# Cosine of h in the first feed-forward: one shifted sine in place of a half-angle sine and its square

## The chip, the cores and the metric

The kernel runs on one core of one Trainium2 chip, in one launch. The metric is device time in microseconds (us), lower is better. The engines are TensorE (PE in the profile, with its weight loads shown apart as PEld), VectorE (DVE), ScalarE (ACT), GpSimd (POOL) and SyncE (SP, which issues most of the DMAs). The kernel before takes 839.35 us, the median of 3 runs (838.67 to 839.87).

## The reference, cut to what matters

The input goes through attention (pooled and local, added up), then two feed-forward blocks. What the change touches is the middle of the first one:

```python
def _moe_ref(x, w_in, w_out):          # x: 2304 x 512, w_in: 512 x 2048, w_out: 2048 x 512
    h = x @ w_in
    g = h * np.cos(h)
    return (g @ w_out).astype(np.float32)
```

The second block computes `(x @ w1) * (x @ w2) @ w3 @ w_out`. All of it is float32.

## The kernel before, in words

**The order of the work is made by a planner, not by hand.** The body of the kernel is written as jobs (Python generators); each step of a job asks for an engine, and `run` (L294) plays a clock of its own: it keeps for each engine the planned end of its last operation, and whenever an engine is free it issues the most urgent step whose inputs are, by the plan, visible. What an operation costs is a formula in `cost` (L104), what it takes until its output can be read is the table `LATENCY`. For ScalarE the formula is (L113 to L115):

```python
load = 1290 if func in (AF.Exp, AF.Sin) and func != table[0] else 0
table[0] = func if load else table[0]
return (45 if not on_chip(ins[0]) else 128 if func == AF.Prelu else 90) + n / 1.2 + load
```

so a 384-column operation costs 365 (in ns) from a PSUM bank and 410 from SBUF, whatever the function, scale and bias. The program that results has one fixed order on every engine; on the chip each engine takes its instructions in that order, and waits where an input is not there yet. A changed cost or a step less can therefore change the order of everything that is issued after it, on all engines.

**The first feed-forward.** 2304 tokens are 6 chunks of 384 columns (N1), the hidden 2048 are 16 blocks of 128 (F1): 96 steps. Every float32 matrix product is made of three passes in the float32r format (a high and a low part of each operand, `mm3`). A step is 12 matmuls for h (`h_job`, L856) into one PSUM bank, then the chain that makes g of it (`chain_job`, L836), then 12 matmuls for y (`y_job`, L883), which add into four banks over the 16 blocks. `LAG = 3` (L56, used in L865) lets h run three steps ahead of y. With the last block of a chunk `y_out_job` (L907) writes y out through ScalarE with `scale=-1.0`, because the chain leaves minus g. There are 32 such copies, as the first two chunks are made in two parts.

**The chain of a step** before the change:

1. ACT: `turns` = h / 2pi as an int32 (rounded)
2. DVE: `c` = h - 2pi * turns
3. ACT: `c` = sin(c / 2)
4. ACT: `c` = (sqrt(2) * c) squared, which is 1 - cos h
5. DVE: `c` = (c - 1) * h, which is -h cos h; the PSUM bank of h is free after it
6. ACT: the high part of g, a copy of `c` as float32r
7. POOL: the low part of g, `c` minus the high part

**Around it.** The start loads and converts the weights (ACT and DVE), does the attention of the first batch and multiplies w3 by w4 of the second block (`ps_w`). From 82 us on the steps of the first feed-forward run, with the attention of the later chunks strewn between them on PE (tiles `ps_s`, `ps_t`, `ps_p`, `ps_sb`, `ps_tb`, `ps_av`). At 557 us the second feed-forward begins (`ps_ab`, `ps_o`); it has no chain. Dummy matmuls that keep PE going (`warm_up`) stop at the first step of h. The first instructions of POOL are memsets of constants (in the block that begins at L1087, the last of them at L1125, `ge.memset(ident, 0.0)`); the four DMAs of the band masks and the two of the identity are issued from ACT's queue.

Of the kernel before, what the change touches and what calls it, by code (L numbers as in the profile page):

```python
# [10 lines left out]
F32 = mybir.dt.float32  # L11
# [4 lines left out]
AF = mybir.ActivationFunctionType  # L16
ALU = mybir.AluOpType
# [5 lines left out]
P = 128  # L23
# [31 lines left out]
TWO_PI = 2.0 * math.pi  # L55
# [24 lines left out]
def fused_kernel(ctx: ExitStack, tc: tile.TileContext, qk_block, v_block, qk_pool, v_pool,  # L80
# [84 lines left out]
    ve, se, pe, ge, sy = (Engine(*e) for e in (("ve", nc.vector), ("se", nc.scalar), ("pe", nc.tensor), ("ge", nc.gpsimd), ("sy", nc.sync)))  # L165
# [8 lines left out]
    const = ctx.enter_context(tc.tile_pool(name="const", bufs=1))  # L174
# [8 lines left out]
    ident = const.tile([P, P], F32, name="ident")  # L183
    ident_r = const.tile([P, P], F32R, name="ident_r")
    bands = const.tile([P, 3, 2 * KS], F32R, name="bands")


    slots = {"t": (tp, 2048, 6), "st": (tp, 4096, 1), "g": (gp, 8 * N1, 3), "c": (gp, 4 * N1, 2), "turns": (gp, 4 * N1, 1),
# [8 lines left out]
    def buf(slot, name, shape, dtype=F32):  # L197

        pool, size, _ = slots[slot[0]]
        item = 8 if dtype == I64 else 4  # L200
        t = pool.tile([P, size // item], dtype, name=name, tag=f"{slot[0]}{slot[1]}", bufs=1)
        t = t[:, :math.prod(shape)]
        if len(shape) == 1:
            return t
        names = "abcd"[:len(shape)]
        return t.rearrange(f"p ({' '.join(names)}) -> p {' '.join(names)}", **dict(zip(names, shape)))
# [6 lines left out]
    def bank(n, name):  # L213

        return psum.tile([P, 512], F32, name=name, tag=f"bank{n}", bufs=1)
# [18 lines left out]
    def on(name, fn, *aps, when=lambda: True):  # L234
        yield name, fn, aps, when
# [5 lines left out]
    def at_hand(name):  # L241
        return sorted(x for x in free[name] if x[0] <= now[0])

    def take(name, n=1, spare=lambda: 0):

        yield from until(lambda: len(at_hand(name)) >= n + spare())
        got = at_hand(name)[:n]
        for x in got:
            free[name].remove(x)
        return got[0][1] if n == 1 else [x[1] for x in got]  # L250
# [15 lines left out]
    def give(name, slot, engine):  # L266
        free[name].append((ends[engine] + LATENCY[engine], slot))

    def give_stored(name, slot, to):

        free[name].append((visible(to), slot))

    def count(key, n=1):
        done[key] = done.get(key, 0) + n

    def reached(key, n):
        return lambda: done.get(key, 0) >= n
# [558 lines left out]
    def chain_job(n, ps, at):  # L836

        turns_slot = yield from take("turns")
        turns = buf(turns_slot, "turns", [N1], I32)
        yield from on("se", lambda: se.activation(out=turns, in_=ps, func=AF.Identity, scale=1.0 / TWO_PI), ps)  # L840
        c_slot = yield from take("c")
        c = buf(c_slot, "c", [N1])
        yield from on("ve", lambda: ve.scalar_tensor_tensor(out=c, in0=turns, scalar=-TWO_PI, in1=ps, op0=ALU.mult, op1=ALU.add), turns)
        give("turns", turns_slot, "ve")
        yield from on("se", lambda: se.activation(out=c, in_=c, func=AF.Sin, scale=0.5), c)
        yield from on("se", lambda: se.activation(out=c, in_=c, func=AF.Square, scale=math.sqrt(2.0)), c)
        yield from on("ve", lambda: ve.scalar_tensor_tensor(out=c, in0=c, scalar=1.0, in1=ps, op0=ALU.subtract, op1=ALU.mult), c)
        give("bank", at, "ve")
        g_slot = yield from take("g")
        g = buf(g_slot, "g", [2, N1], F32R)  # L850
        yield from on("se", lambda: se.copy(g[:, 0, :], c), c)
        yield from on("ge", lambda: ge.tensor_tensor(out=g[:, 1, :], in0=c, in1=g[:, 0, :].bitcast(F32), op=ALU.subtract), g)
        give("c", c_slot, "ge")
        gs[n] = g, g_slot
# [52 lines left out]
    def y_out_job(i, f, e, ps):  # L907
        slot = yield from take("t")
        yt = buf(slot, "yt", [N1])
        yield from on("se", lambda: se.activation(out=yt, in_=ps, func=AF.Copy, scale=-1.0), ps)  # L910
        give(f"bank{4 + e}", 0, "se")
        to = (y_sc if f == F1 - 1 else part_sc)[:, e, i * N1:(i + 1) * N1]
        yield from on("se", lambda: se.dma_start(out=to, in_=yt), yt)
        give_stored("t", slot, to)
        count("stored")
# [171 lines left out]
    with tc.manual_schedule():  # L1087
        z = buf(("turns", 0), "zeros", [WARM])
        ge.memset(z, 0.0)
        zr = z.bitcast(F32R)  # L1090
        warmed = [(bank(7, "ps_z"), True)]

        def warm_up():

            if warmed[0] is None:
                if done.get("w5", 0) < F2 or not at_hand("bank7"):
                    return False
                ps, alone = bank(7, "ps_z"), True
            else:
                ps, alone = warmed[0]  # L1100
            pe.matmul(ps[:, :WARM], lhsT=zr[:, :P], rhs=zr, start=alone, stop=alone)
            ends["pe"] += REST if now[0] > RISEN else 0
            return True

        idle.append(warm_up)

        W5 = 2 * F2
        first, seen = {}, []
        first.update({i: HALF if i == 1 else F1 * i for i in range(NC1)})
        first.update({("f", f): f if f < HALF else f + HALF for f in range(F1)})  # L1110

        def attention(i, at):

            for b in sorted({(UPC * i + m) // UPB for m in range(UPC)} - set(seen)):
                seen.append(b)
                if b < EARLY:
                    for m in range(UPB):
                        Job(at + U_QK + 0.5 * m, unit_qk_job(UPB * b + m))
                for p in range(KC):
                    Job(at + U_PAIR + SLOPE * p, pair_job(b, p))  # L1120
                    Job(at + U_POOL + SLOPE * p, pool_v_job(b, p))
            for m in range(UPC):
                Job(at + U_UNIT + PER_UNIT * m, unit_job(UPC * i + m))

        ge.memset(ident, 0.0)  # L1125
        raw = buf(("st", 0), "bands_raw", [3, 2, KS])
        for half in (slice(0, KS), slice(KS, P)):
            for w in range(2):
                se.dma_start(out=raw[half, :, w], in_=bands_in[w * (QB - KS):, :, w * (KB - KS):][:KS, :, :KS])
        se.dma_start(out=ident[:QB, :QB], in_=ident_in)  # L1130
        se.dma_start(out=ident[QB:, QB:], in_=ident_in[:P - QB, :P - QB])

        se.activation(out=ident_r[:, :1], in_=z[:, :1], func=AF.Exp)
        Job(-50, consts_job(raw))
        ends["sy"] = FIRST
        attention(0, A0)
        for j in range(F2):
            at = j - 1 if j >= 2 else -5.75 + 0.02 * j
            Job(at, w_job(("w4", j), w4[j]))
            Job(at + (0.5 if j >= 2 else 0.01), w_job(("w3", 0, j), w3t[0, j]))  # L1140
        for j in range(F2):
            Job(F2 + j + U_W3, w_job(("w3", 1, j), w3t[1, j]))
        Job(900, w5_job())
        for f in range(F1):
            Job(W5 + first["f", f] + U_WI, w_job(("wi", f), w_in[f]))
            Job(W5 + first["f", f] + U_WO, w_job(("wo", f), w_out[f]))
        Job(899, h_job(W5))
        Job(W5 + 1000.5, y_job())
        attention(1, W5 + first[1] - A1)
        for i in range(2, NC1):  # L1150
            run(reached("h", first[i - 1] + 1 - AHEAD if i > 2 else first[0] + HALF + 1))
            attention(i, W5 + first[i])
            if i == 2:
                for f in range(F2):
                    Job(W5 + first[2] + 4 * f, w12_job(f))
        run(lambda: done.get("h", 0) > first[NC1 - 1] and done.get("w12 begun", 0) == F2)
        at_stack.close()
        p2 = ctx.enter_context(tc.tile_pool(name="p2", bufs=1))
        slots.update({"x2": (p2, 4 * KC * N1, 6), "v": (p2, 4 * NH, 2)})
        free["x"] += [(0.0, ("x2", n)) for n in range(6)]  # L1160
        free["v"] = [(0.0, ("v", n)) for n in range(2)]
        base = W5 + NSTEPS
        for n in range(F2 * NQ // 2):
            Job(base + 2 * n / NQ - 8, back_job(n))
        for n in range(len(steps2)):
            Job(base + n - 6, w5_back_job(n))
        Job(base - 8, y_in_job(0))
        Job(base + 1000, ab_job(base))
        Job(base + 1000.5, o_job(base))
        run(reached("out", NT // P))  # L1170
# [53 lines left out]
```

## Time and profile before

| | |
|---|---|
| median of 3 runs | 839.35 us (838.67 to 839.87) |
| the profiled execution | 842.03 us, of which the span of its records is 840.2 us |
| PE busy, PEld busy | 825.3 us (98%), 750.2 us (89%) |
| DVE, ACT, POOL busy | 512.4 us (61%), 464.2 us (55%), 325.6 us (39%) |
| first h, last y of the first feed-forward | 82 us, 557 us |

How to read it: "busy" is the time in which an instruction of an engine runs. Matmuls overlap, and their ends are modelled, so PE's busy time says that it had something, not how fast it went; the steady pace of its groups says that. Idle time "<-X" in front of an instruction is what it waited for. Almost every instruction has the line L161, that of the planner's helper, so groups are told apart by the names of the tiles. In every stretch the granted TensorE clock is 1.00 of full speed.

### The profile page before, as it was taken

What the parts mean: (1) busy time and instruction counts of PE and PEld (TensorE: products, weight loads), DVE (VectorE), ACT (ScalarE), POOL (GpSimd) and SP (SyncE); (2) the same over time, 40 slices, a digit from 0 to 9 for tenths busy, and PEclk for the clock granted to TensorE, in tenths of its full rate; (3) what the DMA queues carried; (4) which work ended last, traced back from release to release, by engine and by line L of the source; (5) the groups of instructions that cost most, each with busy time, mean ns of one, the idle gap of its engine ahead of it and who ended that gap; (6) DMA issues with size and microseconds to landing.
All of it is one profiled execution on the core that took longest, in us unless ns stands there. A gap on an engine that the chain in (4) does not pass through costs nothing.

```text
span 840.2 us, 15590 instructions
## 1 busy us (share of the span) xinstructions
PE 825.3 (98%) x5972; PEld 750.2 (89%) x5972; DVE 512.4 (61%) x935; ACT 464.2 (55%) x930; POOL 325.6 (39%) x298
## 2 busy tenths in 40 slices
PE   7999999999999999999999999999999999999997
PEld 6545669999899999999999999999999999999996
DVE  4988989997775989467453436424336544463342
ACT  3788988876886787767666566631114311331112
POOL 0103214334362654534543324425336633363332
PEclk9999999999999999999999999999999999999999
DMA  9999896144445653353232258870000510120102
GB/s 286 298 304 299 306 329 214 44 138 132 167 132 171 201 175 107 128 191 126 85 136 89 94 191 347 283 255 14 26 26 14 175 26 26 26 95 20 26 25 76
DMA packets 48923, 121.88 MB, mean 145 GB/s; under 512 B 6480, under 2 KB 10832, under 8 KB 48848
## 3 DMA queue, kind: packets, MB, share of 16 engines
q1 hardware_dynamic: 41952, 112.12, 40.7%
q10 hardware_dynamic: 6896, 8.76, 2.9%
q8 instruction: 47, 0.77, 0.4%
q14 instruction: 28, 0.23, 0.1%
HBM read 93.07 MB, written 27.79 MB: 144 GB/s over the span
## 4 chain that ended last, share of the span: by engine, by line
PE 81%; DVE 8%; DMA 4%; ACT 3%; issue 2%; POOL 0%; ACTq 0%; SPq 0%; DVEq 0%; POOLq 0%
PE ps_ab L161 21%; PE ps_y L161 20%; PE ps_h L161 20%; PE ps_o L161 12%; PE ps_w L161 2%; DVE t L161 2%; DMA raw<-w3t 2%; PE ps_av L161 1%; DVE c L161 1%; PE ps_t L161 1%; PE ps_tb L161 1%; PE ps_sb L161 1%; PE ps_s L161 1%; DMA vr<-v_pool 1%; DVE sc L161 1%
## 5 line engine op out<-in xcount | busy, mean ns | idle before, releaser
L161 PE MATMUL ps_y<-g,wo 128*128 128x384 f32 x1152 | 221.9, 337 | 0.0
L161 PE MATMUL ps_h<-xs,wi 128*128 128x384 f32 x1152 | 221.5, 337 | 0.0
L161 PEld LDWEIGHTS ps_h<-xs,wi 128*128 128x128 f32 x1152 | 200.4, 188 | 3.8 <-issue 3.2
L161 PEld LDWEIGHTS ps_y<-g,wo 128*128 128x128 f32 x1152 | 199.8, 188 | 3.0 <-issue 2.1
L161 PE MATMUL ps_ab<-y,w 128*128 128x384 f32 x1008 | 189.0, 337 | 0.4 <-ACT v L161 0.3
L161 POOL TENSOR_TENSOR g<-c,g 128x384 fp32r<-128x384 f32 x96 | 106.7, 1112 | 206.5 <-ACT g L161 192.1
L161 PEld LDWEIGHTS ps_ab<-y,w 128*128 128x128 f32 x1008 | 177.5, 188 | 8.5 <-POOL v L161 0.9
L161 DVE TENSOR_TENSOR v<-v,ps_ab 128x384 f32<-128x384 f32 x168 | 90.8, 552 | 141.8 <-PE ps_ab L161 74.0
L161 ACT ACTIVATE c<-c 128x384 f32<-128x384 f32 x192 | 100.4, 523 | 42.9 <-DVE c L161 39.0
L161 ACT CAST m<-v 128x384 fp32r<-128x384 f32 x48 | 24.6, 513 | 176.8 <-POOL v L161 176.8
L161 PE MATMUL ps_o<-w,m 128*128 128x512 f32 x432 | 110.9, 393 | 0.0
L161 POOL TENSOR_TENSOR v<-v 128x384 f32<-128x384 f32 x48 | 50.5, 1054 | 126.8 <-DVE v L161 126.8
L161 DVE SCALAR_TENSOR_TENSOR c<-turns,ps_h 128x384 f32<-128x384 int32 x96 | 52.7, 549 | 66.3 <-ACT turns L161 59.3
L161 PEld LDWEIGHTS ps_o<-w,m 128*128 128x128 f32 x432 | 80.1, 188 | 12.5
L161 DVE SCALAR_TENSOR_TENSOR c<-c,ps_h 128x384 f32<-128x384 f32 x96 | 52.7, 549 | 54.6 <-ACT c L161 54.3
L161 ACT CAST g<-c 128x384 fp32r<-128x384 f32 x96 | 49.0, 511 | 38.9 <-DVE c L161 34.4
L161 PE MATMUL ps_w<-w,w 128*128 128x512 f32 x128 | 61.0, 607 | 1.7 <-DVE w L161 1.6
L161 ACT ACTIVATE turns<-ps_h 128x384 int32<-128x384 f32 x96 | 46.7, 486 | 27.3 <-PE ps_h L161 27.1
L161 POOL TENSOR_TENSOR m<-v,m 128x384 fp32r<-128x384 f32 x48 | 49.1, 1025 | 23.7 <-ACT m L161 23.7
L161 POOL TENSOR_TENSOR sc<-sc,bmax 128x1024 f32<-128x1024 f32 x12 | 23.6, 1966 | 68.9 <-DVE bmax L161 52.6
L161 PEld LDWEIGHTS ps_w<-w,w 128*128 128x128 f32 x128 | 22.4, 189 | 23.5 <-issue 19.9
L161 DVE SCALAR_TENSOR_TENSOR t<-raw,t 128x512 int32<-128x512 int32 x48 | 42.8, 902 | 0.2
(90 smaller groups left out, 861.9 us busy)
## 6 DMA issues: line engine op xcount, KB each, us to landing
w_sc<-w SPq DMA_DIRECT2D x56, 256.0 KB, 2.3
w<-w_sc SPq DMA_DIRECT2D x28, 512.0 KB, 6.9
raw<-w SPq DMA_DIRECT2D x24, 512.0 KB, 11.9
qk<-qk_block SPq DMA_DIRECT2D x24, 396.0 KB, 8.5
raw<-w3t SPq DMA_DIRECT2D x16, 512.0 KB, 13.5
raw<-w_in SPq DMA_DIRECT2D x16, 512.0 KB, 7.5
raw<-w_out SPq DMA_DIRECT2D x16, 512.0 KB, 8.5
qkr<-qk_pool SPq DMA_DIRECT2D x12, 576.0 KB
```

The source lines that it names most:

```text
L161: return call(*args, **kw)
```

## The change

The argument of the sine is no longer halved. The turns are counted from a quarter turn on (a bias of 0.25 ahead of the rounding), so the rest lies between -3/4 and 1/4 of a turn; with a bias of a quarter turn in the sine it lies between -1/2 and 1/2, and sin(rest + pi/2) is cos h. The square goes away, the second DVE operation becomes a plain product of two tensors, and y is written with the sign as it is. The two biases are columns of a new tile `quarters`, filled by two memsets at the start of POOL's program.

```diff
+    quarters = const.tile([P, 2], F32, name="quarters")
...
     turns = buf(turns_slot, "turns", [N1], I32)
-    yield from on("se", lambda: se.activation(out=turns, in_=ps, func=AF.Identity, scale=1.0 / TWO_PI), ps)
+    yield from on("se", lambda: se.activation(out=turns, in_=ps, func=AF.Identity, scale=1.0 / TWO_PI, bias=quarters[:, 1:]), ps)
...
     give("turns", turns_slot, "ve")
-    yield from on("se", lambda: se.activation(out=c, in_=c, func=AF.Sin, scale=0.5), c)
-    yield from on("se", lambda: se.activation(out=c, in_=c, func=AF.Square, scale=math.sqrt(2.0)), c)
-    yield from on("ve", lambda: ve.scalar_tensor_tensor(out=c, in0=c, scalar=1.0, in1=ps, op0=ALU.subtract, op1=ALU.mult), c)
+    yield from on("se", lambda: se.activation(out=c, in_=c, func=AF.Sin, bias=quarters[:, :1]), c)
+    yield from on("ve", lambda: ve.tensor_tensor(out=c, in0=c, in1=ps, op=ALU.mult), c)
...
-    yield from on("se", lambda: se.activation(out=yt, in_=ps, func=AF.Copy, scale=-1.0), ps)
+    yield from on("se", lambda: se.activation(out=yt, in_=ps, func=AF.Copy, scale=1.0), ps)
...
+    ge.memset(quarters[:, :1], TWO_PI / 4)
+    ge.memset(quarters[:, 1:], 0.25)
     ge.memset(ident, 0.0)
```

## Rows read from the trace of the kernel before

**Rows 1.** Stretches of the span: length, busy time (instructions) of each engine, clock, DMA

```profile
0.00:82.00 82.00, 74.58 (x715) 46.20 (x716) 61.64 (x126) 58.06 (x138) 13.44 (x13) 1.00 0.97 296
82.00:123.00 41.00, 39.28 (x249) 26.92 (x247) 36.80 (x76) 37.38 (x80) 8.51 (x6) 1.00 0.85 311
123.00:190.00 67.00, 66.33 (x560) 64.88 (x557) 65.60 (x111) 54.91 (x108) 23.91 (x18) 1.00 0.43 144
190.00:345.00 155.00, 154.57 (x1498) 144.87 (x1497) 118.73 (x232) 118.53 (x226) 76.31 (x67) 1.00 0.49 156
345.00:557.00 212.00, 212.00 (x1516) 209.91 (x1515) 104.53 (x177) 130.56 (x261) 87.59 (x83) 1.00 0.50 172
557.00:840.00 283.00, 278.53 (x1446) 257.46 (x1444) 125.14 (x219) 64.75 (x121) 115.81 (x112) 1.00 0.16 51
```

**Rows 2.** Waits of PE from 82 to 345 us, and from 557 us on (last row)

```profile
PE ps_p L161 <- DVE vd L161: 1.7, 1, 1.7
PE ps_tb L161 <- POOL sc L161: 0.7, 1, 0.7
PE ps_t L161 <- DVE sc L161: 0.2, 1, 0.2
...
PE ps_ab L161 <- ACT v L161: 0.3, 2, 0.2
```

**Rows 3.** Chain that ended last, two groups of PE and the end of the last steps

```profile
441.41 2.08 PE ps_y L161 x12
443.49 2.08 PE ps_h L161 x12
...
549.57 8.32 PE ps_y L161 x48
```

**Rows 4.** Groups of instructions by form: ACT and DVE (count, busy us, mean ns)

```profile
L161 ACT ACTIVATE c<-c 128x384 f32<-128x384 f32 x192 | 100.4, 523 | 42.9 <-DVE c L161 39.0 <-DVE t L161 1.5
L161 ACT ACTIVATE turns<-ps_h 128x384 int32<-128x384 f32 x96 | 46.7, 486 | 27.3 <-PE ps_h L161 27.1
L161 ACT ACTIVATE yt<-ps_y 128x384 f32<-128x384 f32 x32 | 14.8, 489 | 9.1 <-ACT yt L161 4.4 <-PE ps_y L161 3.3 <-PE ps_ab L161 0.8
L161 ACT ACTIVATE sd<-ps_s,nm 72x144 f32<-72x144 f32 x32 | 11.6, 370 | 1.1 <-DVE nm L161 1.1
L161 ACT ACTIVATE up<-ps_t 128x144 f32<-128x144 f32 x12 | 3.5, 294 | 0.0
L161 DVE SCALAR_TENSOR_TENSOR c<-c,ps_h 128x384 f32<-128x384 f32 x96 | 52.7, 549 | 54.6 <-ACT c L161 54.3
L161 DVE TENSOR_TENSOR v<-v,ps_ab 128x384 f32<-128x384 f32 x168 | 90.8, 552 | 141.8 <-PE ps_ab L161 74.0 <-ACT w L161 66.0 <-POOL y L161 0.9
```

**Rows 5.** Sines and squares from 82 to 190 us (ACT, groups by form)

```profile
L161 ACT ACTIVATE c<-c 128x384 f32<-128x384 f32 x38 | 19.9, 523 | 3.6 <-DVE c L161 1.5 <-DVE t L161 1.5
```

**Rows 6.** Timeline of the last chain, with PE's last y of the stage (start us, us)

```profile
549.41 8.48 PE L161 MATMUL ps_y<-g,wo 128*128 128x384 f32 x48
...
550.35 0.48 ACT L161 ACTIVATE turns<-ps_h 128x384 int32<-128x384 f32 x1
551.52 1.08 ACT L161 ACTIVATE c<-c 128x384 f32<-128x384 f32 x2 [0.69 <-DVE c L161]
553.94 1.01 POOL L161 TENSOR_TENSOR g<-c,g 128x384 fp32r<-128x384 f32 x1 [1.42 <-ACT g L161]
```

**Rows 7.** Timeline of the start: POOL's memsets, ACT's queue

```profile
0.34 0.10 POOL L1217 MEMSET const-uint8-127<- 128x1 uint8 x1
0.98 0.20 POOL L161 MEMSET ident<- 128x128 f32 x1
3.40 1.44 ACTq L147 DMA_DIRECT2D ident<-ident_in  x2
```

**Rows 8.** Timeline of the two longest waits of PE after 82 us

```profile
120.88 0.69 DVE L161 TENSOR_TENSOR vr<-vr 72x512 f32<-72x512 f32 x1 [2.78 <-DMA vr<-v_pool]
122.51 0.71 PE L161 MATMUL ps_p<-ptp,vd 72*64 72x144 f32 x8 [1.72 <-DVE vd L161]
...
183.83 0.52 ACT L161 CAST g<-c 128x384 fp32r<-128x384 f32 x1 [1.14 <-DVE c L161]
184.48 1.02 POOL L161 TENSOR_TENSOR g<-c,g 128x384 fp32r<-128x384 f32 x1 [6.02 <-ACT g L161]
185.45 2.14 POOL L161 TENSOR_TENSOR sc<-sc,bmax 128x1024 f32<-128x1024 f32 x1
187.65 1.09 PE L161 MATMUL ps_tb<-ident,sc 128*128 128x128 f32 x8 [0.67 <-POOL sc L161]
```

## The prediction

> **What bounds the kernel now.** I read the stretches first, then the waits of PE, then the chain that ended last. Up to 82 us the transfers are the limit: the DMA engines are busy 0.97 of the time [rows 1], and no step of h has begun, so no chain runs there. From 82 us on it is PE. Its idle time, length less busy time, is 1.72 us from 82 to 123, 0.67 from 123 to 190, 0.43 from 190 to 345 and nothing at all from 345 to 557 [rows 1]. Busy time of PE is modelled, so I check the pace too: in the steady part the chain that ended last is twelve matmuls of y, twelve of h, and so on, 2.08 us each and back to back [rows 3]; nothing but PE stands on it. What PE waits for behind 82 us adds up to 1.7 + 0.7 + 0.2 + 0.3 = 2.9 us [rows 2]. That is the whole sum that relief on ACT, or anything else beside PE, can win there unless PE's own work falls, and the change leaves every matmul as it is.
>
> **The change part by part.**
>
> The square goes: 96 ACT operations. The 192 instructions `c<-c` are the sines and squares together, same shape, 523 ns each [rows 4], so 96 x 0.523 = 50.2 us of ACT's busy time.
>
> Two bias operands come, one for the sine and one for the turns. No row shows these forms. The nearest pair is the exponential `sd<-ps_s,nm`, whose bias is a column of a tile, and `up<-ps_t`, which has a scale alone; both read 144 columns of PSUM: 370 against 294 ns, 76 more [rows 4]. They differ in partitions and function as well, so the bounds are 0 and 76; a gain is excluded, as the instruction has one operand more to read. That turns (486) costs what the plain scaled copy `yt` does (489) [rows 4] says that no such price is in it now. I take 76, the only pair that shows one: 96 x 2 x 0.076 = 14.6 us. ACT's balance is -50.2 + 14.6 = -35.6 us. The Trainium skill, ScalarE: Activation LUTs, section What ACT_TABLE_LOAD costs, speaks against the change here: it puts each bias given as a 128 x 1 pointer at about 93 ns on top of an ACTIVATE. The rows show a little less for one bias, and by that estimate the balance would be about -32 us. Either way ACT gets lighter, and ACT is not the bound.
>
> The second DVE operation turns from a three-operand form into a plain product that reads the same PSUM bank: 549 ns before, and 552 ns for `v<-v,ps_ab`, the same form, shape and kind of operands [rows 4]. That is +0.3 us over 96, beside PE: nothing. The copy of y keeps its form, only the constant changes: nothing, for all 32.
>
> The chain gets shorter. Sine and square take 1.08 us as a pair [rows 6]; one sine with its bias would take 0.523 + 0.076 = 0.60, and turns 0.08 more, so g is there 0.40 us sooner. What covers this: h runs three steps ahead of y. It is thinnest at the end of the stage, where no further h stands in between. There the last chain ends at 553.94 + 1.01 = 554.95, and the last of four y steps begins at 549.41 + 3 x 2.08 = 555.65 [rows 6], so g is ready 0.70 us before it is wanted, and PE runs the 48 matmuls in one piece [rows 3]. With the change it is early by 1.10 instead. A chain that was in time gains nothing by being earlier. Were that cover gone, the shorter chain would be worth its 0.40 us once.
>
> Two memsets on POOL stand ahead of the one of the identity. One of 128 x 1 takes 0.10 us [rows 7], so 0.20 at most; the DMAs of the identity begin on ACT's queue at 3.40, when its memset is long over (0.98 + 0.20 = 1.18) [rows 7], so 2.2 us cover it. The first turns wait for these memsets as well, more than 80 us after them. No DMA is added or moved.
>
> The order of the program is the unknown part. The planner counts 410 ns for the square and 145 until its output can be read, and asks nothing for a bias: in its plan each chain loses 0.56 us, on the chip 0.40. From the first chain on, every engine's order may shift. Before it nothing in the plan differs but POOL's first moments. The stretch where ACT is crowded is 82 to 190 us: ACT 92.3 of 108 us busy, and DVE 102.4 [rows 1]. 38 of the sines and squares lie there [rows 5], so 19 squares, 9.9 us. But PE's two waits there hang on others: `ps_p` on the landing of a v_pool transfer at 120.88, which the change doesn't touch; `ps_tb` on the softmax product `sc` on POOL, which stood behind a g on POOL, and that behind the ACT copy of g [rows 8]. Bounds for the order: -2.9 us if every wait vanishes, and on the other side +3.1 as worked out under the rivals.
>
> **Sum.** PE's work 0; weights and start 0; end of the stage 0; the wait of `ps_tb` I take as gone, since a chain stands in it: -0.67 us [rows 8]. Against the profiled execution of 842.03 us this gives 841.4. That execution is 2.7 us over the median of the runs, and 1.8 us of it lie outside its span of 840.2; the same step from the median, 839.35 - 0.67, gives **838.7 us**. A measurement of this kernel can tell about 0.2%, 1.7 us, from no change; this is less.
>
> **Rivals.**
>
> *Every wait goes.* With ACT free sooner, weights are converted sooner, DVE's order in 82 to 190 us loosens and both long waits of PE vanish: 839.35 - 2.9 = 836.5. For it: DVE and ACT are both nearly full there, so one freed slot passes on [rows 1]. Against it: the longer wait ends with a transfer and two DVE operations [rows 8], and DVE keeps all its work.
>
> *Slower: g pushes the attention back on POOL.* The plan thinks g ready about half a microsecond sooner, and more often puts the low part of g ahead of the product `sc` of an attention unit; POOL runs in order, and the transposes `ps_tb` behind it stop PE. It is what happened at 184.48: g took 1.02 us, `sc` 2.14 after it, and PE stood [rows 8]. Each unit so hit costs up to that 1.02 us; two are enough to pass 1.7 us, and three of the twelve units (192 tokens each) give 839.35 + 3.1 = 842.4. Against it: POOL is busy only 23.91 of 67 and 76.31 of 155 us in these stretches [rows 1], and PE usually has h and y steps planned in front of the transposes.
>
> *ACT is not relieved.* If a bias cost far more than its bound, say half a square each, the whole relief would be gone; with PE the bound this is again no change: 839.4, the same case as the forecast for the chances.
>
> **How the numbers follow.** That PE stays the bound and the waits change by little, up or down: 0.58, with its own range 837.7 to 841.0. All waits go: 0.22. POOL's order or a like stall in its place: 0.20. I give the two outer cases so much because an order made anew over some 90 steps can't be read from the old one. So faster by over 0.2% 0.22, within 0.58, slower 0.20. The range takes in both ends and leaves out a part of each outer case: from 836.3, a little beyond all waits, to 842.0, two units late on POOL and some tenths.
>
> **What would show it.** In the profile after: 96 instead of 192 `c<-c`, of some 0.60 us, and turns of 0.56; ACT's busy time near 429 us; DVE the same within 1 us. From 345 to 557 us PE at the old pace, with not one wait. The waits of PE behind 82 us: `ps_p` still there, `ps_tb` shorter or gone. It would be wrong if PE's waits there rose beyond 4.5 us or h began later than at 82 us, or if the steps' 2.08 us changed.

## The result, and the profile after

The changed kernel is slower: 843.84 us, the median of 8 runs (841.40 to 847.85), against 838.99 for the kernel before in 8 runs. The ratio is 1.0062, with a 95% interval of 1.0047 to 1.0077, or some 5.2 us; the two medians lie 4.9 us apart. It lies above the predicted range, which ended at 842.0. The profiled execution took 844.89 us, 1.1 over its median, and that of the kernel before 842.03, 3.0 over 838.99: the two traces differ by 2.9 us and can show no more of the loss than that.

First the same stretches as in [rows 1] (columns as there: length, busy time and instructions of PE, PEld, DVE, ACT and POOL, granted clock of TensorE, DMA share, GB/s):

```profile
0.00:82.00 82.00, 75.60 (x709) 46.99 (x710) 63.15 (x129) 57.54 (x139) 11.46 (x15) 0.98 0.96 294
82.00:123.00 41.00, 41.00 (x251) 28.41 (x250) 38.15 (x75) 38.72 (x79) 8.06 (x7) 1.00 0.91 342
123.00:190.00 67.00, 65.17 (x545) 63.38 (x545) 64.11 (x103) 50.65 (x89) 22.96 (x18) 0.97 0.41 117
190.00:345.00 155.00, 151.54 (x1477) 141.25 (x1475) 119.83 (x230) 107.66 (x190) 73.08 (x64) 1.00 0.49 156
345.00:557.00 212.00, 212.00 (x1518) 209.90 (x1519) 103.37 (x181) 116.61 (x216) 93.04 (x86) 1.00 0.49 171
557.00:840.00 283.00, 281.66 (x1464) 260.53 (x1462) 125.27 (x219) 65.10 (x122) 116.59 (x113) 1.00 0.16 52
```

ACT is lighter, as foreseen. But PE is idle for 1.83 us from 123 to 190 and 3.46 from 190 to 345, where it was idle for 0.67 and 0.43 [rows 1]. From 82 to 123 us it is not idle at all, where it was for 1.72, as its wait for `ps_p` now lies behind 123; over the three stretches this is 5.29 us in place of 2.82. Its granted clock is no longer 1.00 everywhere. From 345 us on nothing is lost. The second feed-forward takes the same time: its first matmul, `ps_ab`, starts at 560.9 us here, and started at 557.7 before (the rows below, a tile's groups with smallest, median and largest duration in ns, then first and last start in us). The span of 843.1 leaves 282.2 us behind that start; before, the span of 840.2 left 282.5. So all of the difference arises ahead of the second block, though the first matmul of h starts 4.1 us earlier than before, at 78.2 in place of 82.3: a late start of h, which the text had named as a sign of being wrong, is not it.

```profile
L161 PE MATMUL ps_ab<-y,w x1008: 331/334/444, 560.9 to 832.1; 128*128 128x384 f32 x168
...
L161 PE MATMUL ps_h<-xs,wi x1152: 333/334/738, 78.2 to 552.4; 128*128 128x384 f32 x192
```

Before:

```profile
L161 PE MATMUL ps_ab<-y,w x1008: 331/334/445, 557.7 to 828.8; 128*128 128x384 f32 x168
...
L161 PE MATMUL ps_h<-xs,wi x1152: 331/334/743, 82.3 to 549.2; 128*128 128x384 f32 x192
```

The waits of PE over the whole span (in total, times, the longest) answer to [rows 2]:

```profile
PE ps_sb L161 <- ACT ident_r L161: 3.3, 1, 3.3
PE ps_p L161 <- DVE vd L161: 1.7, 1, 1.7
PE ps_tb L161 <- DVE bmax L161: 1.3, 1, 1.3
PE ps_t L161 <- DVE sc L161: 1.3, 1, 1.3
...
PE ps_t L161 <- POOL sd L161: 0.7, 1, 0.7
PE ps_ab L161 <- ACT v L161: 0.5, 2, 0.3
```

The `ps_p` wait is still there. The `ps_tb` that stood behind POOL no longer waits for it, but three other transposes wait for DVE and POOL, at other places of the order: one `ps_tb` and one `ps_t` for DVE, one `ps_t` for POOL. Behind 82 us the waits add up to 1.7 + 1.3 + 1.3 + 0.7 + 0.5 = 5.5 us, over the 4.5 that the text had named as a sign of being wrong.

The operations themselves cost what the text said, or a little more (groups by form, as [rows 4]):

```profile
L161 ACT ACTIVATE c<-c,quarters 128x384 f32<-128x384 f32 x96 | 59.2, 617 | 41.7 <-DVE c L161 40.6 <-ACT yt L161 0.6
L161 ACT ACTIVATE turns<-ps_h,quarters 128x384 int32<-128x384 f32 x96 | 55.5, 578 | 53.6 <-PE ps_h L161 52.7 <-ACT c L161 0.2
...
L161 DVE TENSOR_TENSOR c<-c,ps_h 128x384 f32<-128x384 f32 x96 | 52.6, 547 | 34.9 <-ACT c L161 34.7
```

A bias operand costs 617 - 523 = 94 ns on the sine and 578 - 486 = 92 on the turns, against the 76 taken. The product of two tensors is as fast as the form it replaces (547 to 549).

The surprise stands in the first microseconds (timeline, as [rows 7]):

```profile
0.74 0.86 SPq L161 DMA_DIRECT2D qk<-qk_block  x2
...
0.98 0.13 POOL L161 MEMSET quarters<- 128x1 f32 x2
1.05 0.21 POOL L161 MEMSET ident<- 128x128 f32 x1
1.10 5.84 PEld L161 LDWEIGHTS ps_z<-zeros 128*128 128x128 f32 x27 [1.10 <-POOL zeros L161]
...
10.50 0.76 PE L161 MATMUL ps_sb<-bands,ident_r 128*128 128x256 f32 x2 [3.27 <-ACT ident_r L161]
```

Before:

```profile
0.74 0.86 SPq L161 DMA_DIRECT2D qk<-qk_block  x2
...
1.10 7.70 PEld L161 LDWEIGHTS ps_z<-zeros 128*128 128x128 f32 x43 [1.10 <-POOL zeros L161]
...
10.55 0.50 PE L161 MATMUL ps_sb<-bands,ident_r 128*128 128x256 f32 x2 [1.55 <-ACT ident_r L161]
```

The memsets cost nothing on the chip: the memset of the identity starts 0.07 us later than before [rows 7]. But PE has 27 dummy matmuls ahead of its first `ps_sb`; before, it has 43. The order of the instructions is another from the beginning, more than 70 us ahead of the first chain. So the memsets, not the chain, moved the start.

**Why two memsets change the order.** In the code, `load` asks for a slot that has been free for SLACK (L59), 1150 ns of the plan, and the plan's clock stands only where some planned operation ends or a job may go on. Before, the memsets end at 690 and 1101 in the plan, and the next end is ScalarE's, at 3931; so the first load is planned at 3.93 us. With two memsets more, at 134 ns each, the identity's ends at 1369, which is past 1150: the first load is planned at 1.37 us, 2.56 us earlier, and the next loads with it. On the chip the first load is issued at 0.74 us in either. From there on the choices of the planner are made with data that it thinks it has sooner. Its clock then runs further ahead of the chip: the first `ps_sb` is planned at 7.17 us and starts at 10.50 on the chip; before, it is planned at 9.09 and starts at 10.55. (The plan's times come from playing its clock through the code; no trace has them.)

### The profile page after: what moved, and what is told of

The parts are those of the page before. It is cut to its first block, busy times and chain, and to the rows that moved or that the text cites. A ratio compares the mean times of both kernels' runs of the same rounds, so it can differ in the third digit from the quotient of the medians.

```text
span 843.1 us, 15573 instructions
## 1 busy us (share of the span) xinstructions
PE 827.0 (98%) x5956; PEld 750.5 (89%) x5956; DVE 513.9 (61%) x935; ACT 436.5 (52%) x834; POOL 325.2 (39%) x300
## 4 chain that ended last, share of the span: by engine, by line
PE 85%; DVE 5%; ACT 4%; DMA 3%; POOL 1%; issue 1%; SPq 0%; ACTq 0%; DVEq 0%; POOLq 0%
PE ps_h L161 21%; PE ps_y L161 21%; PE ps_ab L161 20%; PE ps_o L161 11%; PE ps_w L161 5%; PE ps_t L161 2%; PE ps_sb L161 2%; PE ps_av L161 1%; DVE bmax L161 1%; PE ps_tb L161 1%; PE ps_s L161 1%; DMA raw<-w_in 1%; DVE sc L161 1%; DMA vr<-v_pool 1%; DMA ident<-ident_in 1%
## 5 line engine op out<-in xcount | busy, mean ns | idle before, releaser
L161 ACT ACTIVATE turns<-ps_h,quarters 128x384 int32<-128x384 f32 x96 | 55.5, 578 | 53.6 <-PE ps_h L161 52.7
L161 ACT ACTIVATE c<-c,quarters 128x384 f32<-128x384 f32 x96 | 59.2, 617 | 41.7 <-DVE c L161 40.6
L161 DVE TENSOR_TENSOR c<-c,ps_h 128x384 f32<-128x384 f32 x96 | 52.6, 547 | 34.9 <-ACT c L161 34.7
L161 DVE SCALAR_TENSOR_TENSOR t<-raw,t 128x512 int32<-128x512 int32 x48 | 40.5, 852 | 0.4
```

Of the source, the lines that this page charges most:

```text
L161: return call(*args, **kw)
```

## The experiments

Two things in the plan were changed, then: its **start** (by the memsets) and its **chain** (a square less, and biases that are not charged for). A third is what the chip executes. The first four runs cross them. All times are medians; ratios are to the kernel before, run beside it on the same chip, with 95% intervals. They are not quite the ratios of the two medians: the two differ by up to 0.0012, so a step of that size between two kernels can't be told from none.

**The start undone** (`e1`). The memsets are issued past the planner:

```diff
-        ge.memset(quarters[:, :1], TWO_PI / 4)
-        ge.memset(quarters[:, 1:], 0.25)
+        nc.gpsimd.memset(quarters[:, :1], TWO_PI / 4)
+        nc.gpsimd.memset(quarters[:, 1:], 0.25)
```

> The changed kernel, but its two memsets are issued without a price in the plan, so the plan's first load is at its old moment (3.93 us of the plan's clock instead of 1.37). Start theory (the loss comes from the plan's start, which the memsets move): about 838.5, like before. Chain theory (the loss comes from the order that a chain without the square gives): about 843.8, like the changed kernel. Chip theory (the loss comes from the bias operands or the new product themselves): about 843.8.

Measured: 841.92 us, ratio 1.0032 (1.0014 to 1.0050). It is between the two: half of the loss is gone, half is there without the new start. No theory had that; the start and the chain each seem to have a share. The order is that of the kernel before up to the first chain. One of the new waits can be read off its timeline (start us, us; what ended the idle time):

```profile
168.88 1.73 PE L161 MATMUL ps_y<-g,wo 128*128 128x384 f32 x9
...
171.64 0.49 ACT L161 ACTIVATE yt<-ps_y 128x384 f32<-128x384 f32 x1 [1.85 <-DMA part_sc<-yt]
...
172.18 0.80 PE L161 MATMUL ps_y<-g,wo 128*128 128x384 f32 x3 [1.57 <-ACT yt L161]
...
184.70 1.09 PE L161 MATMUL ps_tb<-ident,sc 128*128 128x128 f32 x8 [0.79 <-POOL sc L161]
```

PE wants a bank whose content ACT has yet to copy out, and ACT's copy stands behind a store that has not landed. The plan had put these y matmuls where, by its prices, the bank was free. The wait ends with a store, and which moved step made the store late the trace does not show.

**The start alone** (`e2`). The kernel before with the tile and the two memsets, nothing reads them:

```diff
+    quarters = const.tile([P, 2], F32, name="quarters")
...
+        ge.memset(quarters[:, :1], TWO_PI / 4)
+        ge.memset(quarters[:, 1:], 0.25)
```

> The kernel before with the two memsets alone, priced in the plan; sine, square and DVE as they were, the biases are filled and not read. Start theory: about 843.8. Chain theory and chip theory: about 839.2, as 0.2 us of memsets are covered.

Measured: 843.36 us, ratio 1.0056 (1.0036 to 1.0077). Two memsets that nothing reads cost nearly as much as the whole change, 4.7 us by the ratio.

**The chain on the chip alone** (`e4`). The memsets are unpriced, and a step that issues nothing charges the plan for a square, so the order on every engine is that of the kernel before with the squares struck out:

```diff
-        ge.memset(quarters[:, :1], TWO_PI / 4)
-        ge.memset(quarters[:, 1:], 0.25)
+        nc.gpsimd.memset(quarters[:, :1], TWO_PI / 4)
+        nc.gpsimd.memset(quarters[:, 1:], 0.25)
...
+        def square():
+            end = ends["se"] = max(now[0], ends["se"]) + cost("se", "activation", c, [c], AF.Square)
+            written[c.tensor.name] = end, "se"
+
+        yield from on("se", square, c)
         yield from on("ve", lambda: ve.tensor_tensor(out=c, in0=c, in1=ps, op=ALU.mult), c)
```

> The changed chain in exactly the order of the kernel before on every engine: the memsets are not priced, and the plan still charges ScalarE for the square, which is not issued. Start theory and chain theory: 838.3 to 839.4, at best the 0.67 us of the ps_tb wait under the kernel before. Chip theory: about 843.8.

Measured: 838.12 us, ratio 0.9991 (0.9974 to 1.0007). The same kernel was run again later (`e9`):

> The old order without the square once more, to narrow what the square's absence is worth where nothing else changes: 837.5 to 839.6. Theory that it is worth nothing, as no chain was late: ratio 0.999 to 1.001; theory that it is worth a few waits of PE: 0.996 to 0.999.

Measured: 838.32 us, ratio 0.9982 (0.9964 to 0.9999). The mean of the two, 0.9987, is 1.1 us less than before; one interval takes in no change and the other hardly leaves it out. That the bias operands or the product are slow on the chip is out. In the stretches of the first of these runs PE's idle time, length less busy time, is 0.33 us from 123 to 190 and nothing from 190 to 345:

```profile
123.00:190.00 67.00, 66.67 (x556) 65.02 (x555) 65.51 (x109) 51.87 (x93) 23.64 (x18) 1.00 0.42 139
190.00:345.00 155.00, 155.00 (x1505) 145.64 (x1503) 120.34 (x232) 111.98 (x199) 77.17 (x68) 1.00 0.49 157
```

**The new start with the old chain in the plan** (`e5`): the `square` step of `e4`, and the memsets priced as in the change.

> The changed chain with the memsets priced and the square charged in the plan but not issued: the order of the kernel before with memsets alone. Start theory: about 843.5, the square's absence on the chip takes off half a microsecond at most. Chain theory: about 838.7. Chip theory: about 843.8.

Measured: 840.60 us, ratio 1.0021 (1.0007 to 1.0034), between what the theories of the start and of the chain had. The start costs here, too, 2.5 us against `e4`.

**Is it the price of the bias?** `e1` loses to `e4` by 3.8 us, and the only difference is that the plan believes in a shorter chain: 0.56 us shorter, where the chip's is shorter by 0.56 less two biases of 0.09, or 0.37. So the plan was given the price (`e6`, on top of `e1`):

```diff
+            load += 90 * sum(a.tensor.name.startswith("quarters") for a in ins)
             return (45 if not on_chip(ins[0]) else 128 if func == AF.Prelu else 90) + n / 1.2 + load
```

> As the run with the memsets unpriced, but the plan charges 90 ns for each bias operand, so that its ScalarE is nearer to the measured one. If the order without the square loses because the plan thinks ScalarE faster than it is: 838 to 840, near the old order without the square (838.1). If the loss is that of one new order among many, and the price of the bias is not what makes it: anywhere from 838 to 844, most likely about 841.5.

Measured: 838.83 us, ratio 0.9989 (0.9971 to 1.0006). From 1.0032 that is 3.6 us back. In its trace (its lines are numbered one higher, as a line was added) PE waits between 82 and 345 us for a transfer (0.4) and once for 0.2 us, and for nothing else:

```profile
PE ps_av L162 <- DMA vb<-v_block: 0.4, 1, 0.4
PE ps_s L162 <- DVE qkd L162: 0.2, 1, 0.2
```

Half the price (`f3`, 45 in place of 90) and twice (`f4`, 180):

> As the run with the bias priced, memsets unpriced, but 45 ns for each bias operand instead of 90. If the price matters by how true it is: between 838.8 and 841.9, about 840.3. If orders are lots: anything from 838 to 844, on either side of both.

> The same with 180 ns for each bias operand, twice what it costs. If only a too hopeful plan costs: 838 to 839.5, like 90. If a price must be true to serve: 840 or more. If orders are lots: anything from 838 to 844.

Measured: 841.39 us, ratio 1.0023 (1.0002 to 1.0044), with 45; 839.15 us, ratio 0.9992 (0.9977 to 1.0006), with 180. In order of the price, 0, 45, 90, 180: 1.0032, 1.0023, 0.9989, 0.9992. At this start too little costs and too much does not; the interval with 45 only just leaves out 1.

**Is it the start's direction?** The changed chain in the plan of `e4`, with the first load planned at 2.50 us (`e7`) and at 5.20 (`e8`) in place of 3.93:

```diff
-        ends["sy"] = FIRST
+        ends["sy"] = 2500.0
```

> The changed chain, square charged in the plan, memsets unpriced; one number differs from the old order without the square: the plan's first load is at 2.50 us of its clock instead of 3.93. If the loss grows with how much too early the plan thinks the loads are: about 839.4, halfway between 838.1 (3.93) and 840.6 (1.37). If any other order costs, whichever way it is moved: 840 to 843.

> The same with the plan's first load at 5.20 us. If too early is what costs: 837 to 838.1, not slower than at 3.93. If any other order costs, whichever way it is moved: 840 to 843.

Measured: 842.17 us, ratio 1.0021 (1.0006 to 1.0035), at 2.50; 838.51 us, ratio 0.9985 (0.9972 to 0.9999), at 5.20. So not any other order costs. But the time at 2.50 was expected halfway between those at 1.37 and 3.93, and its ratio is that of `e5`, at 1.37: in this row the loss does not grow with the step. The same edit in the kernel before, with no part of the change (`g1`, `g2`):

> The kernel before, no part of the change, with the plan's first load at 2.50 us instead of 3.93. If early first loads cost: 841 to 843, between before and the 843.4 of the memsets alone (1.37). If the start is one lot among many: anything from 838 to 843.

> The kernel before with the plan's first load at 5.20 us. If only early loads cost: 838.5 to 839.5. If the order of the kernel before is a lucky one: 841 or more.

Measured: 842.95 us, ratio 1.0030 (1.0014 to 1.0046), at 2.50; 839.13 us, ratio 0.9985 (0.9972 to 0.9998), at 5.20. For the kernel before, first loads at 1.37 (`e2`), 2.50, 3.93 and 5.20 us give 1.0056, 1.0030, 1 and 0.9985: there, the sooner the plan thinks it loads, the slower.

**Both mended, and one of two.** The changed kernel with its memsets in the plan and the price at 90 (`f2`) or 180 (`g3`); with the price at 90 and the first load at 5.20 (`f1`); with no price and the first load at 5.20 (`g4`). The edits are those of `e6`, `f4` and `e8`.

> The changed kernel with 90 ns charged for each bias operand, its memsets in the plan, so the first load is at 1.37 us of the plan. If the causes add: about 841, the changed kernel less the 3.1 us that the price gave with the old start. If the price was luck: 842 to 845.

> The changed kernel with its memsets in the plan and 180 ns for each bias operand. If the price is what mends the changed kernel: 838.5 to 840, like the 839.2 with 90 ns. If that was one lucky order: 841 to 844.

> The changed kernel with its memsets in the plan as they are, 90 ns charged for each bias operand, and the plan's first load at 5.20 us. If the two causes add and each is mended by a plan that is less hopeful: 838 to 838.9, at or below the kernel before. If any order but the old one costs: 840 to 843.

> The changed kernel with nothing charged for the biases and the plan's first load at 5.20 us. If an unpriced bias costs at every start: 841 to 843. If a late start mends the changed kernel by itself: 838 to 839.5.

Measured: 839.23 us, 0.9990 (0.9970 to 1.0010), for `f2`; 838.66 us, 0.9987 (0.9971 to 1.0003), for `g3`; 840.09 us, 1.0005 (0.9990 to 1.0019), for `f1`; 841.10 us, 1.0012 (0.9999 to 1.0025), for `g4`. `f2` is below both of its expectations, 841 and 842 to 845. `f1` has a time in the range of "any order but the old one costs", but its ratio shows no loss. The ratios of all orders side by side, by the plan's first load and by what it charges for the chain:

| chain in the plan | 1.37 us | 2.50 us | 3.93 us | 5.20 us |
|---|---|---|---|---|
| before, square executed | 1.0056 | 1.0030 | 1 | 0.9985 |
| changed, square still charged | 1.0021 | 1.0021 | 0.9991, 0.9982 | 0.9985 |
| changed, bias free (the change: 1.37) | **1.0062** | | 1.0032 | 1.0012 |
| changed, bias at 45 | | | 1.0023 | |
| changed, bias at 90 | 0.9990 | | 0.9989 | 1.0005 |
| changed, bias at 180 | 0.9987 | | 0.9992 | |

Along the third row a start at 5.20 mends most of the loss; along the first column the price does, and there it mends the start as well, which I had not expected: the two causes do not add in general. No version is clearly faster than the kernel before; the best lie at 0.998 to 0.999, with intervals that reach 1 or nearly so.

**Is it the clock?** The granted clock of TensorE, a mean over each run, goes with the plan's first load: averaged over a kernel's runs it is 0.995 to 0.996 at 1.37, 0.996 to 0.997 at 2.50, 0.998 to 0.999 at 3.93 and 0.998 to 1.000 at 5.20. (The kernel before, at 3.93, has 0.998; the 1.00 of its profile is a favourable execution.) But the clock does not decide the time: `f2` and `g3` have 0.995 and 0.996, no more than the changed kernel's 0.996, and lose nothing, while `e1` and `f3` have 0.998 and lose.

## Why the prediction was wrong

**What bounds the kernel**: right. What differs between the two traces shows as PE's idle time and its clock ahead of 345 us; that ACT has less to do shows nowhere by itself.

**The square and the biases**: right in kind. ACT's busy time fell from 464.2 to 436.5 us, 27.7 less where 35.6 were worked out; 2 x 96 x (0.093 - 0.076) = 3.3 us of the gap are the biases' measured price. Sines, squares and turns alone fall by 100.4 + 46.7 - 59.2 - 55.5 = 32.4 us by their groups; ACT's busy time, which counts once what two overlapping instructions share, falls by less. The Trainium skill, ScalarE: Activation LUTs, section What ACT_TABLE_LOAD costs, has about 93 ns for such an operand; the trace agrees with 92 and 94.

**The direct worth of the shorter chain**: right as far as it can be told. 0.67 us were taken, for the wait of `ps_tb`; the old order without the square measured 0.9987, about 1.1 us, and one of its two intervals takes in none. In the trace of `e4` that wait is gone, as was said.

**Two memsets, covered**: this step failed first. On the chip it holds. But the step asked only what covers them there, and passed over their price in the plan, with the sentence "Before it nothing in the plan differs but POOL's first moments". The plan's clock, with its threshold of 1150 against an end at 1101 or 1369, stands in the code that the text had before it. With the chain otherwise as in the change, this start is worth 1.0062 against 1.0032, 2.5 us; by itself, in the kernel before, 4.7 us.

**The order as "the unknown part"**: the sizes were too small, and its direction was not asked for. The text noted that the plan's chain loses 0.56 us and the chip's 0.40 (0.37 with the measured biases), and drew nothing from the difference. A planner that thinks an engine faster than it is puts consumers where their inputs are not ready, and PE, which runs in order, pays. At the old start this is 1.0032 against 0.9987, 3.8 us, and charging 90 ns brings it back. So -1.1 for the chip, +3.8 for the unpriced bias, +2.5 for the start make +5.2 us, where the bound for the order was +3.1. That the three add up to what was measured is no proof: they are steps from the kernel before over `e4` and `e1` to the change, and such steps always do. Over `e5` in place of `e1` the start is 2.9 us, against the mean of `e4` and `e9`, and the unpriced bias 3.4. That every microsecond is lost in this way no trace shows; the reading rests on the price, which mends it.

**The rival for slower** had the sign and the kind of mechanism, attention behind a chain that the plan thinks ready, but not the place. In the changed kernel PE's new waits are for DVE (1.3 and 1.3 us) more than for POOL (0.7), and in `e1` one is for a store. One of them (timeline of DVE, POOL and PE in the changed kernel):

```profile
311.55 1.91 DVE L161 TENSOR_SCALAR bmax<-bmax 128x16 f32<-128x16 f32 x1
...
311.73 0.74 POOL L161 TENSOR_TENSOR w<-t,w 128x256 fp32r<-128x256 f32 x1
...
312.42 1.00 POOL L161 TENSOR_TENSOR g<-c,g 128x384 fp32r<-128x384 f32 x1
...
313.66 1.02 DVE L161 SCALAR_TENSOR_TENSOR sc<-ps_sb,bands 128x256 f32<-128x256 f32 x3
...
314.16 0.41 PE L161 MATMUL ps_t<-ident,sd 72*72 72x72 f32 x4 [1.27 <-DVE sc L161]
```

A DVE operation on 16 columns takes 1.91 us while POOL runs two products, and PE's transposes stand behind what follows it. The plan allows for such a standstill of DVE beside POOL only where DVE writes more than 64 columns (`held`, L100).

**What stays open.** Why the start no longer costs where the bias is priced, and by which of the many moved steps an early plan loses, the runs do not show; each profile is one execution, and single waits come and go between orders. Nor does PE's idle time in a single trace follow the ratios: from 82 to 345 us it is 2.8 us in the kernel before, 2.2 in `e2` (1.0056), 0.8 in `f3` (1.0023) and 1.9 in `g3` (0.9987). That too hopeful a plan costs rests on the table: of the eight orders with a first load at 1.37 or 2.50, or with the bias free or at 45, in which neither 90 nor 180 is charged, none is below 1.0012 (start at 5.20, bias free) and all others are at 1.0021 or above; of the eight others that were tried, none is above 1.0005. This sorting was made with the times known, and the gap between the two groups is smaller than half an interval (that of 1.0012 takes in 1); it is the sixteen together that bear it out, not a single pair. It also has an exception that it does not explain: a start at 1.37 with the bias at 90 or 180 is as hopeful at the start and loses nothing.

## What to carry to other kernels

Where a planner orders the program, a change has two prices: what it does on the chip, and what the plan believes of it. Give each new operation and operand its measured price in the plan before judging it, and look whether any planned time crosses a threshold in the planner, even at the first microsecond. To tell the two apart, keep the order and change the instructions (a step that charges and issues nothing), then keep the instructions and change the order.

## What the runs showed of the hardware

PE's clock can fall after PE has waited, and what follows is slow. In stretches of 4 us of the changed kernel, the first behind the wait of 3.27 us at the start, the others around and behind that of `ps_p` (columns as above, the clock third from the end):

```profile
12.00:16.00 4.00, 4.00 (x62) 3.54 (x59) 1.81 (x3) 2.17 (x4) 0.00 (x0) 0.75 1.02 399
128.00:132.00 4.00, 2.61 (x14) 2.45 (x15) 3.97 (x10) 2.89 (x6) 0.00 (x0) 0.76 1.08 326
132.00:136.00 4.00, 4.00 (x20) 4.00 (x20) 3.92 (x5) 2.87 (x6) 2.16 (x1) 0.82 0.99 233
```

And the timeline of PE there:

```profile
129.39 0.71 PE L161 MATMUL ps_p<-ptp,vd 72*64 72x144 f32 x8 [1.71 <-DVE vd L161]
130.03 3.92 PE L161 MATMUL ps_h<-xs,wi 128*128 128x384 f32 x12
```

After a wait of 1.71 us for `ps_p`, twelve matmuls of h take from 130.03 to 133.78, when the next group starts: 3.75 us instead of 2.08, most of them at the lower of the two levels, 1.2 GHz instead of 2.4 (the granted clock is 0.52, 0.50 and 0.50 in the three microseconds from 130 to 133). In the kernel before the wait of `ps_p` is as long, 1.72 [rows 8], and there the granted clock stays at 1.00 [rows 1]. So a wait can cost its length once more, or not; the 1.7 us here are no part of PE's idle time, and a sum of waits misses them. Why the clock fell behind one of two equal waits, the runs do not show.

The 1.91 us of the small DVE operation above are the other surprise: the median of the 12 of its kind is 168 ns (smallest, median and largest in the row below). It ends 0.04 us after the second of POOL's two products. Of the other eleven, one is slow too, and it also begins while POOL runs a product:

```profile
L161 DVE TENSOR_SCALAR bmax<-bmax x12: 157/168/1906, 25.3 to 394.7; 128x16 f32<-128x16 f32 x12
...
393.71 1.91 POOL L161 TENSOR_TENSOR sc<-sc,bmax 128x1024 f32<-128x1024 f32 x1 [2.15 <-DVE bmax L161]
394.68 0.97 DVE L161 TENSOR_SCALAR bmax<-bmax 128x16 f32<-128x16 f32 x1
```

The Trainium skill, Advanced Engine Details and Errata, section Mode Summary, says that DVE's second port to SBUF is shared with GpSimd, and that GpSimd's instructions and those of DVE that use both ports block each other; the rows fit that, but no row shows which ports this operation uses, and no run here took POOL's work away.
